# Attention's long steps in another order, and the scaling by the row sums split between ScalarE and GpSimd

## The chip, the cores and the metric

The kernel is one launch on one core of a Trainium2 chip. The metric is the device time of that launch in microseconds (us); the median of three runs of the kernel before is 765.63 us (763.31 to 770.97).

Engine names in the rows: PE is TensorE (PEld its weight loads), DVE is VectorE, ACT is ScalarE, POOL is GpSimd, SP is the engine that issues most of the DMAs (SPq its queue).

## What is computed

The reference is one attention over 16 heads (2 batches of 8, 768 positions, head size 64) whose mask comes from hashing, and behind it two feed-forward layers:

```
q_bits = (q @ proj) > 0                  # 6 bits for each row; k_bits alike
mask   = bucket(q_bits) == bucket(k_bits)
scores = where(mask, scale * q @ k.T, -1e9)
attn   = exp(scores - max(scores)) / (sum + 1e-9)
x      = attn @ v                        # 1536 rows of 512
x      = relu(x @ w_in)**2 @ w_out       # 512 -> 2048 -> 512
out    = silu(x @ w2_in) @ w2_out
```

The change lies in the attention alone: in the order of the steps that make the hash bits, and in the division of `attn @ v` by the row sums.

## The kernel before, in words

The heads are taken in 8 pairs. A pair gives 4 units (a head and one half of its 768 query rows), a unit gives 3 score tiles of 128 query rows by 768 keys. One loop, `for d in range(-5, 99)`, runs over the 96 score tiles, one for each step d, and everything is issued in the order in which it is written there: each engine works through its own list in that order and waits where an operand or a buffer is not ready. A tile that is scored in step d is reduced and put through the exponential in step d+1, transposed some steps later and multiplied with V four transposed tiles behind that. A step of the usual kind is, in order:

- VectorE: `row_max` of the last score tile (L639), `t_lo` of the last transposed tile of the step before (L678), two small operations `row_live` (L643, L644), and in some steps a piece of the preparation of four weight blocks (`w_exp`, `w_sign`, `w_low`: L597, L601, L605);
- TensorE: 6 transposes of probability blocks (`transp`, L667); ScalarE copies them out of PSUM as rounded values (`t_hi`, L672), VectorE writes the remainders (`t_lo`);
- TensorE: two times `av`, each a product of V with a rounded tile and with its remainder (L691, L692); every sixth `av` is followed by a ScalarE copy (L697) and two DMAs;
- ScalarE: the exponential of the last score tile (`score_exp`, L652);
- TensorE: the next score tile (`score_mm`, L634): four products of 384 columns, two of 128 rows and two of 76 rows. The latter hold the hash bits among their rows.

One step in twelve is a **long step** (d = 5, 17, 29, 41, 53, 65, 77). It also holds `bits_mm` of the next pair, 12 products of 384 columns (L522), and `bits_cmp` on VectorE (L527), whose result SP copies by two small DMAs into the operands of the score tiles (L558). The first score tile that needs these bits is the one that is scored two steps on. From d = 17 a long step also holds `rb_mm` (L714): 6 transposes that spread the reciprocals of the row sums of an earlier pair over 128 partitions, and `x_norm` (L723), a VectorE product of them with the pair's result. Step 92 holds `rb_mm` and `x_norm` alone. A score tile, the bits and the spread sums each take one of two PSUM buffers in turn.

At the end of a long step up to 65, ScalarE scales the queries of the pair after next (`scale_q`, L487), and GpSimd issues two DMAs of that pair (`load_hi`, L481, L482). GpSimd's list goes on with `x_put` of the normalised pair (L731 to L741), the remainders of V and of the next operands (L571, L572, L507), blocks of the weights (L614 to L623), the spreading of the next sums (L706), the sum of two halves of the result (`x_sum`, L719) and, two steps ahead of steps 5, 29, 53 and 77, the limiting of a weight block (`w_limit`, L593), which VectorE's `w_exp` in that long step reads. The feed-forward layers follow, ordered by a planner (`Plan`) that the change does not touch.

The calls in a long step:

```
extra[d0 + 5].append((bits_mm, bits_cmp, p))          # d0 = 12 * (p - 1)
extra[k].append((rb_mm, x_norm, p))                   # k = 12 * (p + 1) + 5
held = [(dve, pe(p), p) for pe, dve, p in more]       # both on TensorE at once
```

## Time and profile before

| | us |
|---|---|
| median of 3 runs (lowest, highest) | 765.63 (763.31, 770.97) |
| the profiled execution | 766.11 |
| its span, first to last instruction | 764.3 |
| TensorE busy in it | 743.0 (97%) |
| VectorE busy | 594.6 (78%) |
| ScalarE busy | 452.9 (59%) |
| GpSimd busy | 399.2 (52%) |

Attention takes about the first 255 us of the span, the feed-forward layers the rest. A busy TensorE is not one that is never held up: its products overlap, each is listed longer than the distance to the next, and short waits hide between them. The waits that matter here are read instruction by instruction in the timeline, where a bracket behind a row names the idle time ahead of it and what ended it.

### The profile page before, as it was taken

To read this page: it belongs to the slowest core of one execution; us is meant where nothing else is said; L and a number is where in the kernel's file an instruction comes from. 1 tells how busy PE (TensorE), PEld (TensorE's weight loads), DVE (VectorE), ACT (ScalarE), POOL (GpSimd) and SP (SyncE) were. 2 spreads that over 40 slices of the span, in tenths; PEclk is the share of its full clock that TensorE was granted. 3 is DMA by queue.
4 is the path that set the end of the run, shared out by engine and by line. 5 is a ranking of instruction groups with operands and counts; after the bars stand their busy time and mean duration, and the time that the engine had idled before them with its cause. 6 is when DMAs were issued, how large, how long until landed. Compare 5 with 4: busy or idle time off the path is not lost.

```text
span 764.3 us, 10886 instructions
## 1 busy us (share of the span) xinstructions
PE 743.0 (97%) x3746; PEld 630.2 (82%) x3747; DVE 594.6 (78%) x1054; ACT 452.9 (59%) x850; POOL 399.2 (52%) x290
## 2 busy tenths in 40 slices
PE   7899999999999989999999999999999999999998
PEld 3688988989988868888888888888788888888887
DVE  4789999999999799758747967899974875585542
ACT  1788888888879667367267339546634625623520
POOL 0544554864654574763564662867567255455200
PEclk8999999999999999999999999999999999999999
DMA  7787886886851402221221211202222031121012
GB/s 180 210 186 180 218 185 163 215 199 157 204 131 37 164 28 83 83 82 53 87 68 70 68 72 40 72 27 70 98 83 83 21 117 32 53 96 42 1 69 97
DMA packets 30054, 78.79 MB, mean 103 GB/s; under 512 B 4552, under 2 KB 9032, under 8 KB 30000
## 3 DMA queue, kind: packets, MB, share of 16 engines
q1 hardware_dynamic: 25808, 66.69, 30.2%
q0 software_dynamic: 4032, 11.01, 6.1%
q8 instruction: 30, 0.49, 0.3%
q10 hardware_dynamic: 160, 0.39, 0.3%
q14 instruction: 24, 0.20, 0.1%
HBM read 51.42 MB, written 3.15 MB: 71 GB/s over the span
## 4 chain that ended last, share of the span: by engine, by line
PE 76%; DVE 16%; DMA 3%; ACT 2%; issue 1%; POOL 0%; SPq 0%; ACTq 0%; DVEq 0%
PE bank L336 32%; PE bank L255 16%; PE bank L226 9%; PE s L634 6%; PE t L667 5%; DVE mt L639 3%; DVE tl L678 3%; PE o L691 3%; PE o L692 3%; PE bs L522 2%; DVE ys L149 2%; DVE xb L155 1%; ACT P L652 1%; DVE wt L173 1%; DVE wt L172 1%
## 5 line engine op out<-in xcount | busy, mean ns | idle before, releaser
L170 POOL TENSOR_SCALAR wt<-wt 128x512 f32<-128x512 f32 x56 | 116.9, 2097 | 45.3 <-ACT wt L168 45.3
L155 POOL TENSOR_TENSOR wp<-wt,wp 128x512 fp32r<-128x512 f32 x56 | 76.5, 1376 | 96.2 <-ACT wp L153 96.2
L255 PE MATMUL bank<-xb,wp 128*128 128x512 f32 x480 | 111.3, 390 | 3.8 <-DVE xb L155 2.2
L652 ACT ACTIVATE P<-s,mt 128x768 f32<-128x768 f32 x96 | 95.7, 997 | 28.3 <-DVE mt L644 25.8
L255 PEld LDWEIGHTS bank<-xb,wp 128*128 128x128 f32 x480 | 89.7, 188 | 24.0 <-DVE xb L155 2.6
L678 DVE TENSOR_TENSOR tl<-t,th 128x384 fp32r<-128x384 f32 x192 | 104.9, 548 | 3.0 <-ACT th L672 2.7
L639 DVE TENSOR_REDUCE mt<-s 128x1 f32<-128x768 f32 x96 | 91.3, 951 | 13.4 <-PE s L634 13.0
L153 ACT CAST wp<-wt 128x512 fp32r<-128x512 f32 x56 | 34.6, 620 | 105.6 <-DVE wt L173 64.4
L672 ACT CAST th<-t 128x384 fp32r<-128x384 f32 x192 | 82.2, 483 | 20.7 <-PE t L667 20.6
L634 PE MATMUL s<-kk,qq 76*128 76x384 f32 (+1 forms) x384 | 86.6, 345 | 7.4 <-DMA kk<-lp 2.9
L667 PE MATMUL t<-ident,P 128*128 128x128 f32 x576 | 81.5, 274 | 2.2 <-DVE tl L678 2.2
L260 DVE TENSOR_TENSOR ts<-bank,ts 128x512 f32<-128x512 f32 x80 | 54.7, 690 | 37.0 <-PE bank L255 34.4
L226 PE MATMUL bank<-x0h,wp 128*128 128x512 f32 x256 | 80.2, 390 | 0.0
L634 PEld LDWEIGHTS s<-kk,qq 76*128 76x128 f32 (+1 forms) x384 | 68.4, 191 | 12.0 <-issue 7.6
L667 PEld LDWEIGHTS t<-ident,P 128*128 128x128 f32 x576 | 67.7, 140 | 9.7 <-DVE tl L678 4.6
L691 PE MATMUL o<-th,vv 128*128 128x384 f32 x192 | 72.6, 378 | 0.0
L692 PE MATMUL o<-tl,vv 128*128 128x384 f32 x192 | 64.5, 336 | 0.0
L240 ACT ACTIVATE ts<-bank 128x512 f32<-128x512 f32 x48 | 28.5, 593 | 52.2 <-PE bank L226 26.7
L226 PEld LDWEIGHTS bank<-x0h,wp 128*128 128x128 f32 x256 | 48.1, 188 | 9.9
L155 DVE TENSOR_TENSOR gql<-ts,gqh 128x512 fp32r<-128x512 f32 x64 | 46.2, 733 | 12.3 <-ACT gqh L153 12.1
L172 DVE SCALAR_TENSOR_TENSOR wt<-raw,wt 128x512 uint32<-128x512 uint32 x58 | 51.5, 890 | 0.6
L168 ACT ACTIVATE wt<-raw 128x512 f32<-128x512 f32 x58 | 38.7, 670 | 20.5 <-POOL wp L155 11.0
(144 smaller groups left out, 1694.6 us busy)
## 6 DMA issues: line engine op xcount, KB each, us to landing
raw<-in_dram SPq DMA_DIRECT2D x64, 512.0 KB
qq<-hq SPq DMA_DIRECT2D x32, 192.0 KB
kk<-in_dram POOLq DMA_DIRECT2D x14, 384.0 KB, 4.8
rq<-in_dram SPq DMA_DIRECT2D x8, 384.0 KB
rk<-in_dram SPq DMA_DIRECT2D x8, 384.0 KB
qq<-lp SPq DMA_DIRECT2D x16, 192.0 KB
kk<-lp SPq DMA_DIRECT2D x16, 192.0 KB
vr<-in_dram SPq DMA_DIRECT2D x8, 384.0 KB
```

What stands on the lines that cost most here:

```text
L155: add(("DVE", "POOL")[pool], l, lambda: eng.tensor_tensor(out=lo(), in0=src(), in1=hi().bitcast(F32), op=ALU.subtract), (*rk, *hk), lk)
L170: add("DVE" if fast else "POOL", 0.5 if fast else 2.4, lambda: eng.tensor_scalar(out=wtt, in0=wtt, scalar1=W_LO, scalar2=W_HI, op0=ALU.max ...
L226: mm(bank[b], w[:, x, op, sl], t["x0"][y][:, kt], start=kt == 0 and j == 0, stop=kt == 3 and j == 2)
L255: mm(bank[b], w[:, p, op, k * 128 : k * 128 + 128], x[:, q, xop, k], start=first and k == 0 and j == 0, stop=k == 1 and j == 2, skip_group ...
L336: mm(bank[b][:, 0:wd], x, y, start=i == 0 and n == 0, stop=i == FB - 1 and n == 2)
L634: mm(s[:, n, 0:QW], t["qq"][h][0:kk, ab, c0 : c0 + 128], t["kk"][h][0:kk, ab, n * QW : (n + 1) * QW], start=ab == 0, stop=ab == 1)
L639: nc.vector.tensor_reduce(out=m[:, 0:1], in_=s[:, :, 0:QW], op=ALU.max, axis=AX.XY, negate=True)
L652: nc.scalar.activation(out=e.rearrange("p (a b) -> p a b", a=2), in_=s[:, :, 0:QW], func=AF.Exp, scale=m[:, 1:2], bias=m[:, 2:3], accum_ou ...
L667: nc.tensor.transpose(t[:, j * 128 : (j + 1) * 128], P[u, j][:, kt * 128 : (kt + 1) * 128], ident)
L678: nc.vector.tensor_tensor(out=tl, in0=t[:, 0:QW], in1=th.bitcast(F32), op=ALU.subtract)
L691: mm(o[:, 0:QW], vv, th, start=kt == 0, stop=False)
L692: mm(o[:, 0:QW], vv, tl, start=False, stop=kt == KT - 1)
```

## The change

The two PSUM buffers become two fixed tiles, and a variable says which one comes next. In a long step TensorE now takes the first `av` ahead of the bits, the next score tile straight behind the bits, then the second `av`, and `rb_mm` last, in the buffer that the bits had. Score tile and bits have the same buffers as before the change relative to one another: the score tile goes into the buffer whose exponential is done in this step. `x_norm` is no longer a VectorE product that reads PSUM; ScalarE copies the spread sums from PSUM to SBUF (into the tile `rw` from which they came), and GpSimd multiplies.

```diff
-    ps_s = att.enter_context(tc.tile_pool(name="ps_s", bufs=2, space=PSUM))
+    ps_s = att.enter_context(tc.tile_pool(name="ps_s", bufs=1, space=PSUM))
+    ss = [ps_s.tile([128, 2, 512], F32, tag=f"s{i}", name=f"s{i}") for i in range(2)]
+    parity = [0]
...
     def score_mm(u, j):
-        s = ps_s.tile([128, 2, 512], F32, tag="s", name=f"s{u}_{j}")
+        s = ss[parity[0]]
+        parity[0] ^= 1
...
     def x_norm(s, p):
-        ta = xs[p][0].rearrange("p (a b) -> p a b", a=2)
-        nc.vector.tensor_tensor(out=ta if p < 4 else x_rows(p).rearrange("p (a b) -> p a b", a=2), in0=s[:, :, 0:QW], in1=ta, op=ALU.mult)
+        rb = rows[p].rearrange("p c h d -> p (c h d)")
+        nc.scalar.copy(out=rb.rearrange("p (a b) -> p a b", a=2), in_=s[:, :, 0:QW])
+        ta = xs[p][0]
+        nc.gpsimd.tensor_tensor(out=ta if p < 4 else x_rows(p), in0=rb, in1=ta, op=ALU.mult)
...
-            held = [(dve, pe(p), p) for pe, dve, p in more]
-            for dve, t, p in held[:1]:
-                dve(t, p)
-            for n in (g - V_LAG, g + 1 - V_LAG):
-                if 0 <= n < G:
-                    av(n)
-            for dve, t, p in held[1:]:
-                dve(t, p)
+            old = [n for n in (g - V_LAG, g + 1 - V_LAG) if 0 <= n < G]
+            for n in old[0 : 1 if more else 2]:
+                av(n)
+            for pe, dve, p in more[:1]:
+                dve(pe(p), p)
             if ready and not more:
                 score_exp(*ready, m)
+            if more:
+                parity[0] ^= 1
             u, j = divmod(d + 5, 3)
             if u < NU:
                 new = u, j, score_mm(u, j)
+            if more:
+                for n in old[1:]:
+                    av(n)
+            for pe, dve, p in more[1:]:
+                dve(pe(p), p)
```

TensorE in step 41, before, from the last of the 12 products of the bits (`bs4`) to the first transpose of step 42; `rb2` are the spread sums, `o13` the two `av`, `s15_1` the next score tile:

```order
L522 MATMUL bs4_1791<-lp4_1492,pjh_92 48x384
L714 MATMUL rb2_1804<-ident_89,rw2_1700 128x128 x6
L691 MATMUL o13_1813<-th78_1711,vv3_1375 128x384
L692 MATMUL o13_1813<-tl78_1713,vv3_1375 128x384
L691 MATMUL o13_1813<-th79_1719,vv3_1375 128x384
L692 MATMUL o13_1813<-tl79_1734,vv3_1375 128x384
L634 MATMUL s15_1_1819<-kk3_1_1452,qq3_1_1451 128x384 x4
L667 MATMUL t84_1839<-ident_89,P14_0_1688 128x128
```

The same engine and step in the changed kernel, where `s0` holds first the bits and then the spread sums, and `s1` the score tile; the first two rows stand ahead of the bits:

```order
L695 MATMUL o13_1741<-th78_1663,vv3_1336 128x384
L696 MATMUL o13_1741<-tl78_1665,vv3_1336 128x384
...
L525 MATMUL s0_89<-lp4_1450,pjh_94 48x384
L638 MATMUL s1_90<-kk3_1_1411,qq3_1_1410 128x384 x4
L695 MATMUL o13_1741<-th79_1671,vv3_1336 128x384
L696 MATMUL o13_1741<-tl79_1685,vv3_1336 128x384
L718 MATMUL s0_89<-ident_91,rw2_1652 128x128 x6
L671 MATMUL t84_1787<-ident_91,P14_0_1641 128x128
```

One `av` has moved ahead of the bits, the score tile ahead of the other, and the spread sums to the end of the step.

ScalarE in the changed kernel, from the exponential of step 41 to that of step 42; before, the same list had no COPY of `rw2`:

```order
L656 ACTIVATE P15_0_1739,sums3_1439<-s1_90,mt_96 128x768
L727 COPY rw2_1652<-s0_89 128x768
L490 ACTIVATE rq5_1547<-rq5_1547 128x768
L676 CAST th84_1791<-t84_1787 128x384
L676 CAST th85_1799<-t85_1795 128x384
L656 ACTIVATE P15_1_1805,sums3_1439<-s1_90,mt_96 128x768
```

The copy of the spread sums stands ahead of `scale_q` (`rq5`), and both stand ahead of the two casts `t_hi` of step 42.

GpSimd in the changed kernel, from `x_sum` of step 39 to `x_put` of step 42; before, the same list had no product of `rw2` and `ta2`:

```order
L723 TENSOR_TENSOR ta2_1268<-ta2_1268,tb2_1269 128x768
L729 TENSOR_TENSOR ta2_1268<-rw2_1652,ta2_1268 128x768
L484 DMA hq5_1778<-rq5_1547 128x768
L485 DMA hk5_1779<-in_1_dram 128x768
L737 CAST x0h_61<-ta2_1268 128x512
```

The product stands ahead of the two DMAs of `load_hi` and of all that GpSimd does up to the next long step.

## Rows read from the trace of the kernel before

**Rows 1.** The chain that ended last, the page's shares by engine.

```profile
PE 76%; DVE 16%; DMA 3%; ACT 2%; issue 1%; POOL 0%; SPq 0%; ACTq 0%; DVEq 0%
```

**Rows 2.** Timeline of PE, score tiles of two usual steps: start, length, engine, line, operands, count.

```profile
140.01 0.86 PE L634 MATMUL s<-kk,qq 128*128 128x384 f32 x4
142.07 0.86 PE L634 MATMUL s<-kk,qq 128*128 128x384 f32 x4
```

**Rows 3.** Timeline of PE in steps 41 to 43.

```profile
124.36 0.82 PE L667 MATMUL t<-ident,P 128*128 128x128 f32 x6
125.37 0.37 PE L522 MATMUL bs<-hq,pjh 128*48 128x384 f32 x1 [0.19 <-ACT P L652]
...
127.49 0.81 PE L714 MATMUL rb<-ident,rw 128*128 128x128 f32 x6
...
128.85 0.94 PE L634 MATMUL s<-kk,qq 128*128 128x384 f32 x4
129.63 0.82 PE L667 MATMUL t<-ident,P 128*128 128x128 f32 x6
...
134.11 0.59 PE L634 MATMUL s<-kk,qq 76*128 76x384 f32 x2 [0.55 <-issue]
```

**Rows 4.** Timeline of DVE in steps 41 and 42.

```profile
127.69 1.07 DVE L527 TENSOR_SCALAR bt<-bs,pcr 48x768 fp32r<-48x768 f32 x1 [0.46 <-PE bs L522]
128.69 0.94 DVE L723 TENSOR_TENSOR ta<-rb,ta 128x768 f32<-128x768 f32 x1
...
131.35 0.55 DVE L678 TENSOR_TENSOR tl<-t,th 128x384 fp32r<-128x384 f32 x1
```

**Rows 5.** Timeline of ACT in steps 41 and 42.

```profile
127.19 0.83 ACT L487 ACTIVATE rq<-rq 128x768 f32<-128x768 f32 x1
130.21 0.86 ACT L672 CAST th<-t 128x384 fp32r<-128x384 f32 x2 [2.19 <-PE t L667]
131.47 0.99 ACT L652 ACTIVATE P<-s,mt 128x768 f32<-128x768 f32 x1 [0.39 <-DVE mt L644]
```

**Rows 6.** Timeline of PE, steps 19, 31, 55, 67: second half of the score tile.

```profile
75.97 0.59 PE L634 MATMUL s<-kk,qq 76*128 76x384 f32 x2 [0.60 <-DMA qq<-bt]
...
105.20 0.58 PE L634 MATMUL s<-kk,qq 76*128 76x384 f32 x2 [0.33 <-issue]
...
163.21 0.59 PE L634 MATMUL s<-kk,qq 76*128 76x384 f32 x2 [0.23 <-issue]
...
192.27 0.59 PE L634 MATMUL s<-kk,qq 76*128 76x384 f32 x2 [0.69 <-issue]
```

**Rows 7.** Timeline of SP in step 41, and one stretch of step 17 (DMA share, GB/s last).

```profile
129.62 0.77 SPq L558 DMA_DIRECT2D kk<-bt  x1
...
72.00:73.00 1.00, 1.00 (x9) 1.00 (x8) 1.00 (x3) 0.86 (x2) 0.92 (x2) 1.00 0.99 203
```

**Rows 8.** Timeline of POOL, steps 41 and 50 to 52.

```profile
128.43 0.59 POOL L481 DMA_DIRECT2D hq<-rq  x1 [4.74 <-PE rb L714]
...
130.38 1.29 POOL L732 TENSOR_TENSOR x0l<-ta,x0h 128x512 fp32r<-128x512 f32 x1
...
149.57 0.82 POOL L706 COPY rw<-ri 128x768 f32<-128x768 f32 x1 [1.18 <-DVE ri L704]
150.36 1.82 POOL L719 TENSOR_TENSOR ta<-ta,tb 128x768 f32<-128x768 f32 x1
152.72 1.92 POOL L593 TENSOR_SCALAR wi<-wi 128x512 f32<-128x512 f32 x1 [0.54 <-ACT wi L589]
```

**Rows 9.** Timeline of DVE in step 53.

```profile
155.01 0.42 DVE L597 TENSOR_SCALAR wi<-wi 128x512 uint32<-128x512 uint32 x1
...
157.12 1.07 DVE L527 TENSOR_SCALAR bt<-bs,pcr 48x768 fp32r<-48x768 f32 x1 [0.50 <-PE bs L522]
```

**Rows 10.** Timeline of POOL and of DVE in the feed-forward part.

```profile
276.40 2.84 POOL L155 TENSOR_TENSOR xb<-ys,xb 128x1024 fp32r<-128x1024 f32 x1
...
277.02 2.77 DVE L173 SCALAR_TENSOR_TENSOR wt<-raw,wt 128x512 uint32<-128x512 uint32 x1
```

More of the change, by code (lines that the diff above doesn't have):

```diff
@@ L516, in bits_mm @@
         t = pair[p]
-        s = ps_s.tile([128, 2, 512], F32, tag="s", name=f"bs{p}")
+        s = ss[parity[0]]
         hp, lp = t["hp"], t["lp"]
@@ L537, in bits_first @@
         t = pair[0]
-        s = ps_s.tile([128, 2, 512], F32, tag="s", name=f"bf{i}")
+        s = ss[i]
         c0 = 72 * i
@@ L629, in score_mm @@
         t = pair[p]
-        s = ps_s.tile([128, 2, 512], F32, tag="s", name=f"s{u}_{j}")
+        s = ss[parity[0]]
+        parity[0] ^= 1
         c0 = z * QW + j * 128
@@ L710, in rb_mm @@
     def rb_mm(p):
-        s = ps_s.tile([128, 2, 512], F32, tag="s", name=f"rb{p}")
+        s = ss[parity[0]]
         for c in range(6):
```

## The prediction

> **What bounds the kernel now.** I read the chain of waits first: TensorE carries 76% of it and VectorE 16% [rows 1]. Then the timeline of one usual attention step: score tiles start 2.06 us apart on TensorE [rows 2], and TensorE has nothing to wait for between them. Eight products of 384 columns and six transposes make up such a step. The twelve products of the bits start at 125.37 and the next instruction at 127.49 [rows 3], so a product takes 0.177; eight take 1.42 and six transposes the other 0.64.
>
> Then a long step, d = 41 [rows 3 to 5]. The reader should see four things. The bits wait for the exponential that frees their buffer (bracket 0.19), so the transposes end 0.37 ahead of them (124.36 + 0.64 = 125.00, bits at 125.37). The next score tile waits for `bits_cmp`: 127.69 + 1.07 = 128.76 on VectorE, and the tile, listed as 0.94 instead of 0.86, is held 0.08, to 128.93. ScalarE has 2.19 idle behind `scale_q`. And two steps on, the second half of the score tile, the half that needs the bits, waits again: bracket 0.55, with "issue" as its releaser. In step 19 the same place names the DMA `qq<-bt` [rows 6]; I take it as that DMA in all five. A listed product overlaps the next by some 0.16 (0.33 against 0.177), so the real wait is the bracket plus 0.16: 0.76 behind step 17, 0.49 behind 29, 0.71 behind 41, 0.39 behind 53, 0.85 behind 65 [rows 3, 6]. Behind step 77 no such wait stands in the timeline.
>
> So a long step is closed by a chain that TensorE's order does not set: bits, compare, small DMA, score tile. Work that is saved inside it only lengthens the wait at its end, unless the DMA comes earlier too.
>
> **The order on TensorE.** One `av` (0.35) moves into the gap ahead of the bits: 125.00 + 0.35 = 125.35, and the bits still start at 125.37. They end at 127.49; the score tile takes 4 x 0.177 to 128.20, since its buffer's exponential is over; the second `av` ends at 128.55. The spread sums wait for the compare, to 128.93, and end at 129.57. The transposes of step 42 start there instead of at 129.63 [rows 3]: 0.06 gained. The bubble has only moved from in front of the bits to in front of the spread sums.
>
> **VectorE** loses seven products of 0.94 [rows 4], 6.6 us in all. None of it is on the path by itself: in step 41 the product ran while TensorE worked on the score tile that VectorE needed next.
>
> **ScalarE** gains seven copies of 128x768 out of PSUM. No row shows one. Two casts of 384 columns out of PSUM take 0.86 together, `scale_q` over 768 columns takes 0.83, the exponential 0.99 [rows 5]. I take 0.83, the like operation without a table of exponents, and keep 0.70 and 0.99 as ends. An instruction starts some 0.07 before the listed end of the one ahead of it (128.76 and 128.69 in [rows 4]; I use the same on ScalarE). The copy starts 0.20 behind the transposes (as `bits_cmp` behind the bits), at 129.77; `scale_q`, now behind it, at 130.53; the casts of step 42 at 131.29. They were at 130.21, so they come **1.08 later**. Who waits for them: VectorE's remainder, from about 131.76 to 132.33 (0.55 long, [rows 4]), and by it the PSUM buffer that the second three transposes of step 43 take. TensorE gets there at 129.57 + 2.06 + 0.32 = 131.95 and is held until 132.35: **0.40 lost**. From there 0.32 of transposes, 0.71 of `av` and 0.35 of score tile put the half that needs the bits at 133.73. Without its wait it stood at 134.11 - 0.71 = 133.40. So what is taken from its wait is 0.71 - 0.33 = 0.38, if the DMA has landed by then.
>
> **The DMA.** In step 41 GpSimd issues the two big copies of `load_hi` from 128.43 on [rows 8], and SP issues the second small copy of bits at 129.62 [rows 7]: the small ones queue among the big ones, and in step 17 the DMA engines are 99% busy at that time [rows 7]. In the changed kernel `load_hi` stands behind the product on GpSimd. The copy ends at 130.60; the product, priced by `x_sum` of the same shape, takes 1.82 [rows 8]; so `load_hi` starts at about 132.5, **4.07 later**. The small DMAs then run almost alone, and I take it that they land by 133.7. Gains by the same sum: 0.43 behind step 17, 0.16 behind 29, 0.38 behind 41, 0.52 behind 65. Step 77 has no `scale_q` and keeps the 0.06.
>
> **GpSimd's backlog.** All that GpSimd does up to the next long step comes 4.07 later. In five periods it has several us idle before its next `rw`, and this is hidden. Between 41 and 53, where the sums of the weight blocks are made, its idle time is 1.18 ahead of `rw` and 0.54 ahead of `w_limit` [rows 8], 1.72 in all. `w_limit` is then 2.35 late: it starts at 155.07 and ends at 156.99. VectorE's `w_exp` stood at 155.01 [rows 9] and would come at some 157.07, 2.06 later; behind it on VectorE stand the remainder and `bits_cmp`, which had 0.50 to spare. `bits_cmp` is 1.56 late, and the spread sums, the bits' DMA and the score tile with it. The half in step 55 comes at 163.21 - 0.39 + 0.33 + 1.56 = 164.71: 1.50 lost, and the 0.38 of step 41 is spent waiting.
>
> **The sum**: -0.43 - 0.16 + 1.50 - 0.52 - 0.06 = +0.33. Step 5 has no `x_norm`; in step 92 the spread sums move by one `av` and the copy fits between casts: below 0.1 either way. The profiled execution took 766.11, so 766.4; the median of the runs shown lies 0.5 lower, so **766.0**.
>
> **Rivals.**
> *GpSimd is not late in step 53* (its idle time is rough, and 1.7 of 4.07 is known to be there): the 1.50 falls away and 0.44 comes in: -1.6, median scale 764.0. For it: VectorE needs `w_limit` in four long steps only, and three have idle time enough. Against: the list up to step 53 shows no other gap.
> *The bits' DMA lands no earlier*: no gain behind 17, 29, 41 and 65, and 1.56 more in step 53: +1.5, 767.1. For it: the row names "issue", not the DMA, in four of five places. Against: step 77, the one with no `load_hi`, has no wait.
> *GpSimd's product holds VectorE (slower).* One row shows such a thing: a product on words took 2.77 on VectorE while GpSimd ran one from 276.40 to 279.24, and it ended just behind it [rows 10]. If the remainder of step 42 were held like this until the product ends, at 132.5, the second transposes would slip by 0.74 in each of seven long steps: +5.2, 771.2 with the rest. It decides if the remainder cannot start beside the product. Against: the remainder at 131.35 took its usual 0.55 [rows 4] while GpSimd ran a product from 130.38 to 131.67 [rows 8].
> The Trainium skill (SBUF — State Buffer, the notes under its diagram of ports) has a rule against more work on GpSimd: it shares a pair of ports with VectorE under an exclusive lock, and a VectorE operation with two SBUF inputs waits for a whole GpSimd instruction that reads SBUF. By that rule the row at 277.02 is held and the remainder, with one input in PSUM, is not; the trace agrees with both.
>
> **Chances.** The forecast 0.52, GpSimd in time 0.20, the DMA no earlier 0.20, VectorE held 0.05, something not seen 0.03. The copy's ends move the 0.40 by -0.13 to +0.16 in five steps, -0.6 to +0.8. The runs before lay between 763.31 and 770.97, so a median of a few can be off by 1 to 2. From 764.0 less 1.4 to 767.1 plus 1.9: 762.6 to 769.0. A change of under 1% (7.7 us) can't be told from none; all waits that the change could take away make 3.2 us, so faster by that 0.02; slower only if VectorE is held for more than I priced, 0.04; within 1% 0.94.
>
> **What would show it.** `w_limit` ending behind 156 us and `w_exp` of step 53 behind it; the casts behind a long step a good 1 us later against the transposes; no wait in the second half of the score tiles of steps 19, 31, 43 and 67; `load_hi` some 4 us later. I am wrong if the remainders beside the product are longer than 0.55, if those waits stay, or if VectorE, relieved of 6.6 us, shortens the usual steps below 2.06.

## The result, and the profile after

The changed kernel took **772.71 us** (median of 12 runs, 768.9 to 777.26) beside 766.14 for the kernel before (12 runs, 763.31 to 771.22): ratio **1.0081, 95% interval 1.0062 to 1.0100**, 6.2 us slower. The forecast was 766.0 with a range of 762.6 to 769.0. A change of under 1% either way was what I held likeliest (0.94), and that came true; but the time is outside the range.

In the kernel after, `score_mm` is L638, `row_max` L643, `t_hi` L676, `t_lo` L682, `av` L695 and L696, `rb_mm` L718, `x_sum` L723, the copy on ScalarE L727, the product on GpSimd L729, V's split L574 and L575, `w_limit` L596, `w_exp` L600. Its profiled execution took 770.77, span 769.0. Of its page, the busy times and the chain by engine:

```profile
PE 745.4 (97%) x3747; PEld 630.8 (82%) x3747; DVE 591.4 (77%) x1047; ACT 457.0 (59%) x857; POOL 411.5 (54%) x297
...
PE 75%; DVE 11%; DMA 4%; POOL 3%; ACT 2%; SPq 2%; issue 2%; ACTq 0%; DVEq 0%; POOLq 0%
```

VectorE lost 5 points of the chain [rows 1], and GpSimd, which had none, has 3. That is the result in one line: work was taken from an engine with little slack and given to one that has idle time, but whose list now makes TensorE wait.

The timeline of PE in steps 41 to 43, which answers to [rows 3]:

```profile
124.51 0.82 PE L671 MATMUL t<-ident,P 128*128 128x128 f32 x6
...
125.53 0.37 PE L525 MATMUL s<-hq,pjh 128*48 128x384 f32 x1
...
127.65 0.86 PE L638 MATMUL s<-kk,qq 128*128 128x384 f32 x4
...
129.07 0.84 PE L718 MATMUL s<-ident,rw 128*128 128x128 f32 x6 [0.20 <-DVE bt L530]
129.75 0.82 PE L671 MATMUL t<-ident,P 128*128 128x128 f32 x6
...
131.80 0.49 PE L671 MATMUL t<-ident,P 128*128 128x128 f32 x3
132.55 0.55 PE L671 MATMUL t<-ident,P 128*128 128x128 f32 x3 [0.26 <-DVE tl L682]
...
133.65 0.86 PE L638 MATMUL s<-kk,qq 128*128 128x384 f32 x4
```

This stretch went as forecast. The bracket ahead of the bits is gone and stands ahead of the spread sums; the second three transposes are held (they start 0.75 behind the first three instead of 0.33, so 0.42 is lost); and the score tile of step 43 is one unbroken row of four products: the wait of 0.55 for the bits is gone, as are those of steps 19, 31, 55 and 67 [rows 6].

What went wrong is on GpSimd. ScalarE, and then GpSimd's list from step 41 on, which answers to [rows 5] and [rows 8]:

```profile
130.00 0.80 ACT L727 COPY rw<-s 128x768 f32<-128x768 f32 x1 [2.57 <-PE s L718]
130.69 0.85 ACT L490 ACTIVATE rq<-rq 128x768 f32<-128x768 f32 x1
131.44 0.85 ACT L676 CAST th<-t 128x384 fp32r<-128x384 f32 x2
```

```profile
130.94 1.84 POOL L729 TENSOR_TENSOR ta<-rw,ta 128x768 f32<-128x768 f32 x1 [7.51 <-ACT rw L727]
132.72 0.61 POOL L484 DMA_DIRECT2D hq<-rq  x1
...
147.49 0.83 POOL L574 CAST vv<-vr 128x768 fp32r<-128x768 f32 x1
148.39 1.80 POOL L575 TENSOR_TENSOR vv<-vr,vv 128x768 fp32r<-128x768 f32 x1
150.16 1.84 POOL L510 TENSOR_TENSOR lp<-rk,hk 128x768 fp32r<-128x768 f32 x1
...
152.57 0.84 POOL L710 COPY rw<-ri 128x768 f32<-128x768 f32 x1
153.36 1.85 POOL L723 TENSOR_TENSOR ta<-ta,tb 128x768 f32<-128x768 f32 x1
155.34 1.92 POOL L596 TENSOR_SCALAR wi<-wi 128x512 f32<-128x512 f32 x1
```

From 130.94 to 157.26 GpSimd does not pause. `w_limit` ends at 157.26 (forecast 156.99). But V's split, in the middle of this list, ends at 150.19, and TensorE wants V first. In the kernel before, the same split ended at 146.01:

```profile
144.18 1.83 POOL L572 TENSOR_TENSOR vv<-vr,vv 128x768 fp32r<-128x768 f32 x1
```

TensorE in steps 50 and 29, and in step 29 what it waited for on VectorE and GpSimd:

```profile
150.25 0.45 PE L695 MATMUL o<-th,vv 128*128 128x384 f32 x1 [2.73 <-POOL vv L575]
...
99.79 0.84 PE L718 MATMUL s<-ident,rw 128*128 128x128 f32 x6 [1.72 <-DVE bt L530]
```

```profile
97.04 0.43 DVE L600 TENSOR_SCALAR wi<-wi 128x512 uint32<-128x512 uint32 x1 [2.02 <-POOL wi L596]
```

```profile
93.29 1.82 POOL L723 TENSOR_TENSOR ta<-ta,tb 128x768 f32<-128x768 f32 x1 [2.97 <-DMA tb<-ob]
95.09 1.92 POOL L596 TENSOR_SCALAR wi<-wi 128x512 f32<-128x512 f32 x1
```

In step 29 the idle time that I had counted as slack was a wait for a DMA: `x_sum` stands ahead of `w_limit` and waits for `tb`. SP issued that DMA at 87.20, and it took 6.1 us to be used instead of 3.5 in the kernel before:

```profile
89.27 0.60 SPq L699 DMA_DIRECT2D tb<-ob  x1
...
92.78 1.84 POOL L719 TENSOR_TENSOR ta<-ta,tb 128x768 f32<-128x768 f32 x1 [0.53 <-issue]
```

The DMA engines are fuller at this time. DMA share and GB/s (the last two columns) of the kernel after, six us on either side of the issue, and of the kernel before, five us at the same place:

```profile
81.00:87.00 6.00, 6.00 (x42) 5.70 (x40) 5.89 (x15) 5.66 (x14) 4.65 (x4) 1.00 1.19 255
87.00:93.00 6.00, 6.00 (x41) 5.72 (x40) 5.84 (x17) 5.32 (x13) 0.82 (x1) 1.00 1.17 228
```

```profile
83.00:88.00 5.00, 5.00 (x36) 4.91 (x35) 5.00 (x12) 4.65 (x12) 0.64 (x1) 1.00 0.75 233
88.00:93.00 5.00, 5.00 (x36) 4.88 (x35) 4.96 (x16) 4.46 (x11) 1.04 (x2) 1.00 0.86 194
```

I put this down to `load_hi`, which comes late and so runs together with what is behind it. The traces show each copy landing in 16 parts. By 4.17 us behind the issue half of the parts of this `tb` had landed, instead of by 2.60 in the kernel before. In the ten traces with `load_hi` at its old place this took 2.5 to 3.4; in the ten where it came late, 3.6 to 4.7 (3.57 in b_hi2, which has the old order and the old scaling), but 2.95 in e3. So a late `load_hi` does go with a later copy. The last part can also be late alone. In b_w16 (below), with `load_hi` at its old place, 15 parts landed by 3.01 and the sixteenth at 4.26, and `x_sum` waited for it:

```profile
92.28 0.60 SPq L699 DMA_DIRECT2D tb<-ob  x1
...
97.17 1.84 POOL L719 TENSOR_TENSOR ta<-ta,tb 128x768 f32<-128x768 f32 x1 [1.91 <-DMA tb<-ob]
```

The section on the tail has what stood in front of it.

**A ledger.** The start of the same weighted sum (`av`) on TensorE, counted from the bits of step 5 and compared with the kernel before, in us (plus is later); e1 is the order alone, e2 the split alone, e8 the changed kernel with two edits (all below):

| weighted sum of step | 9 | 21 | 30 | 39 | 51 | 63 | 75 | 81 | 96 |
|---|---|---|---|---|---|---|---|---|---|
| the change | -0.12 | -0.53 | +1.07 | +1.69 | +4.34 | +4.42 | +3.94 | +4.09 | +4.61 |
| e1 | +0.17 | +0.74 | +0.69 | +0.95 | +1.13 | +1.46 | +1.42 | +2.25 | +2.32 |
| e2 | -0.32 | -1.18 | -1.09 | -0.62 | +0.64 | +1.13 | +0.18 | +0.83 | +1.06 |
| e8 | -0.11 | -0.53 | +0.74 | +1.29 | +0.95 | +2.58 | +2.07 | +2.77 | +3.29 |

The last weighted sum is 4.6 us later, and the part behind it is longer by 1.58 (511.14 instead of 509.56 to the end): 6.2 together, the 0.81% of the runs. The stretch ahead of step 5 is left out: ScalarE waits there for a weight block's DMA, and TensorE behind it, by anything from nothing to 5 us in the profiles of this study. b_w16 had it longest:

```profile
37.79 0.66 ACT L589 ACTIVATE wi<-raw 128x512 f32<-128x512 f32 x1 [5.02 <-DMA raw<-in_dram]
```

So single profiles of two kernels are compared from step 5 on. Even then a row is good to some us only: e14 (below) differs from e8 by three warm-up products ahead of step 5, and its last entry is +6.72 where e8's is +3.29.

### The profile page after: what moved, and what is told of

Read it like the earlier page. It is cut to its first block, busy times and chain, and to the rows that moved or that the text cites. A ratio compares the mean times of both kernels' runs of the same rounds, so it can differ in the third digit from the quotient of the medians.

```text
span 769.0 us, 10902 instructions
## 1 busy us (share of the span) xinstructions
PE 745.4 (97%) x3747; PEld 630.8 (82%) x3747; DVE 591.4 (77%) x1047; ACT 457.0 (59%) x857; POOL 411.5 (54%) x297
## 4 chain that ended last, share of the span: by engine, by line
PE 75%; DVE 11%; DMA 4%; POOL 3%; ACT 2%; SPq 2%; issue 2%; ACTq 0%; DVEq 0%; POOLq 0%
PE bank L336 32%; PE bank L255 17%; PE bank L226 8%; PE t L671 5%; PE s L638 5%; PE o L695 2%; PE o L696 2%; DVE ys L149 2%; PE s L525 2%; DVE tl L682 2%; DVE mt L643 1%; DMA kk<-lp 1%; DVE xb L155 1%; DVE bt L530 1%; DMA raw<-in_dram 1%
## 5 line engine op out<-in xcount | busy, mean ns | idle before, releaser
L682 DVE TENSOR_TENSOR tl<-t,th 128x384 fp32r<-128x384 f32 x192 | 104.6, 547 | 10.7 <-ACT th L676 10.4
L643 DVE TENSOR_REDUCE mt<-s 128x1 f32<-128x768 f32 x96 | 91.2, 950 | 11.9 <-PE s L638 10.9
L638 PE MATMUL s<-kk,qq 76*128 76x384 f32 (+1 forms) x384 | 85.3, 343 | 5.6 <-DMA kk<-lp 3.4
L676 ACT CAST th<-t 128x384 fp32r<-128x384 f32 x192 | 82.7, 488 | 6.7 <-PE t L671 6.7
L638 PEld LDWEIGHTS s<-kk,qq 76*128 76x128 f32 (+1 forms) x384 | 68.7, 191 | 9.4 <-issue 5.4
L695 PE MATMUL o<-th,vv 128*128 128x384 f32 x192 | 72.8, 379 | 2.7 <-POOL vv L575 2.7
L696 PE MATMUL o<-tl,vv 128*128 128x384 f32 x192 | 64.5, 336 | 0.0
```

The lines of the kernel that those rows point to most:

```text
L638: mm(s[:, n, 0:QW], t["qq"][h][0:kk, ab, c0 : c0 + 128], t["kk"][h][0:kk, ab, n * QW : (n + 1) * QW], start=ab == 0, stop=ab == 1)
L643: nc.vector.tensor_reduce(out=m[:, 0:1], in_=s[:, :, 0:QW], op=ALU.max, axis=AX.XY, negate=True)
L676: nc.scalar.copy(out=th, in_=PT[g][0][:, 0:QW])
L682: nc.vector.tensor_tensor(out=tl, in0=t[:, 0:QW], in1=th.bitcast(F32), op=ALU.subtract)
L695: mm(o[:, 0:QW], vv, th, start=kt == 0, stop=False)
```

## The experiments

Three theories: **1**, GpSimd's late and longer list; **2**, the order on TensorE; **3**, ScalarE's copy in front of the casts.

### The two halves

e1, the order alone (against the changed kernel), and e2, the split alone (the kernel before with the new `x_norm`):

```diff
 # e1, in x_norm
-        nc.scalar.copy(out=rb..., in_=s[:, :, 0:QW])
-        nc.gpsimd.tensor_tensor(out=..., in0=rb, in1=ta, op=ALU.mult)
+        nc.vector.tensor_tensor(out=..., in0=s[:, :, 0:QW], in1=ta, op=ALU.mult)
```

> The new order of the long step alone: the scaling by the sums is VectorE's product out of PSUM again, as before. Theory 1 (the loss is GpSimd's: its list starts late behind ScalarE's copy and is longer by the product): within 1 us of the kernel before, 765.3 to 767, no wait for V in step 50 and no wait for w_limit in step 29. Theory 2 (the order on TensorE costs it, rb's transposes being last in the step): 770 to 773, near the changed kernel. Theory 3 (ScalarE's copy and what stands behind it on ScalarE): 765 to 767 as well.

> The copy on ScalarE and the product on GpSimd alone, in the order of the long step before. Theory 1: slower by 3 to 7 us (769 to 773), with GpSimd's list late in the same steps, the wait for V in step 50 between 1 and 3 us and waits for w_limit in steps 29, 53 or 77. Theory 2: as before, 765 to 767. Theory 3: 768 to 772, but with the time in waits for the casts on ScalarE, and none for GpSimd.

Measured: e1 768.77 (ratio 1.0044, 1.0023 to 1.0064), e2 769.03 (1.0039, 1.0016 to 1.0063). Neither half is free. e2 came as theory 1 expects, at the low end, with a wait of 1.42 for V, and VectorE waiting 0.61 and 1.12 for `w_limit` in steps 29 and 77; no wait for ScalarE's casts is in it that the kernel before did not have, which is against theory 3. e1 lies above what theory 1 gave it and below theory 2, so neither theory alone is the whole. In e1 no wait for V or `w_limit` is left, as expected, but TensorE is held behind every long step. DVE and PE of e1 in step 42:

```profile
130.24 0.96 DVE L727 TENSOR_TENSOR ta<-s,ta 128x768 f32<-128x768 f32 x1 [1.08 <-PE s L718]
```

```profile
132.67 1.10 PE L671 MATMUL t<-ident,P 128*128 128x128 f32 x6 [0.46 <-DVE tl L682]
```

The spread sums are last in the step, so VectorE stands idle for 1.08 until they are there, and the maximum and the remainder queue behind the product. Before, the product followed `bits_cmp` at once [rows 4]. There are six such holds, with brackets of 0.40 to 0.46. A bracket leaves out the overlap of two listed products; by the starts, a hold is 0.76 to 0.82 (0.20 of it ahead of the second three transposes), 4.7 in all. In return the waits for the bits two steps on, 3.2 before, are down to 0.5, because TensorE gets there later. The difference, 2.0, is most of the 2.32 of the ledger's row, and 0.83 of it comes behind step 77, where the kernel before had no such wait to lose.

That the two halves add up to the change's 1.0081 does not mean that each keeps its price in it: in the change the same hold is 0.42, since ScalarE and not VectorE takes the spread sums.

### Where GpSimd's list starts

e3 puts the product on VectorE behind ScalarE's copy; e4 issues `scale_q` and `load_hi` ahead of copy and product; e15 leaves GpSimd's product out for the first four pairs.

```diff
 # e3
-        nc.gpsimd.tensor_tensor(out=..., in0=rb, in1=ta, op=ALU.mult)
+        nc.vector.tensor_tensor(out=..., in0=rb, in1=ta, op=ALU.mult)
 # e4, ahead of the loop over more[1:]
+            if more:
+                for fn, a in [x for x in todo[d] if x[0] in (scale_q, load_hi)]:
+                    fn(*a)
+                todo[d] = [x for x in todo[d] if x[0] not in (scale_q, load_hi)]
 # e15
+        if p >= 4:
             nc.gpsimd.tensor_tensor(out=x_rows(p), in0=rb, in1=ta, op=ALU.mult)
```

> The changed kernel with its product on VectorE, out of SBUF after ScalarE's copy; GpSimd has no product. This parts the two halves of theory 1. If it is the product's own 1.84 us on GpSimd and its wait for the copy: the wait of 2.73 us for V in step 50 falls under 1 us, w_limit is no longer waited for, and the time is 766 to 769. If GpSimd's list is late because of the load of hi, which waits for the scaling of q that stands behind the copy on ScalarE: the V wait stays at 1.5 to 2.7 us and the time at 769 to 772. Theories 2 and 3: 770 to 773, since the order and ScalarE's copy are as in the changed kernel.

> The changed kernel with the scaling of q and the load of hi put ahead of the copy and the product in the long step. Theory 1 with the product as the cause: V is still about 2.7 us late in step 50 since the product still stands ahead of it; the holds for the landing of tb in steps 29 and 77 go, if the later load of hi is what crowds the DMA engines there, and the waits in the second halves of steps 19, 31 and 67 come back (0.3 to 0.7 us each): 768.5 to 771. Theory 3: the casts are waited for less by 0.4 us in each of six steps, 768 to 770, with the V wait unchanged.

> The changed kernel without GpSimd's product for the first four pairs (their rows go on unscaled; the copy on ScalarE and all else stays). GpSimd's list then starts with the load of hi, which still waits for the scaling of q behind the copy: at 131.5 instead of 132.7 in step 41's period. If the list's start and length make V's wait: 2.73 falls by about 1.2 to 1.5 us, and the time to 770 to 771.5. If V's wait is made by something else, it stays at 2.7 and the time at 772.7.

Measured: e3 776.32 (1.0142, 1.0120 to 1.0164), e4 768.35 (1.0035, 1.0015 to 1.0055), e15 771.70 (1.0075, 1.0046 to 1.0103). For V the profiles give a clean series, counted from the start of the bits of step 41:

| | `load_hi` issued | V ready | TensorE waits for V |
|---|---|---|---|
| before | 3.05 | 20.64 | none |
| e1, order alone | 3.05 | 21.89 | none |
| e2, split alone | 5.76 | 23.29 | 1.42 |
| e4 | 3.05 | 23.66 | 1.32 |
| e15, no product | 6.41 | 23.93 | 1.99 |
| the change | 7.19 | 24.67 | 2.73 |

Ready less wait, V is wanted at 21.9 where it is waited for (22.3 in e4): the kernel before had 1.3 us of slack there, and 4 us were taken. The order alone takes 1.25 of them: in e1 GpSimd's `x_put` waits 1.28 for the product that now comes last in the step. So e1 has no wait, e2 has 1.42, and the two together have 2.73. Without the product (e15) the list starts 0.78 earlier and V comes 0.74 earlier. I had expected 1.2 to 1.5; the load started 0.40 behind the end of the scaling, with a cast as its releaser. With `load_hi` at its old place and the product kept (e4), V comes 1.01 earlier. So either one alone keeps V 3.0 to 3.3 later than before, since both wait for ScalarE's copy of the spread sums; they overlap and do not add up. The time of e15 cannot be told from the change's.

Of the kernels that keep the split and the new order, e4 alone is clearly faster than the change. It is just below what theory 1 gave it and inside what theory 3 did. V's wait is half of the 2.7 that I had expected, TensorE's wait for `w_limit` is gone, and so are the five holds for the remainders (0.42 each by the starts), since the casts now stand behind the copy alone. That is what theory 3 said of the casts. Against it, the waits for the bits came back (1.55 in step 19, 0.65 in 43, 0.63 in 67). e4 together with an earlier V was not run. e3 missed: GpSimd is relieved, but TensorE waits 1.30 to 1.36 behind each long step:

```profile
137.10 1.10 PE L671 MATMUL t<-ident,P 128*128 128x128 f32 x6 [1.36 <-DVE tl L682]
```

Copy and product one behind the other on the engines that split the tiles are the dearest form of the scaling; by the ratios, the place on GpSimd saves 0.6% against it.

### V and the sum of x earlier or later on GpSimd

e5 moves V's split to d0+7, ahead of the second load of kk; e6 also `w_abs` and `w_limit` a step earlier; e7 puts V's split behind that load; e8 is e7 with `x_sum` a step later.

```diff
 # e5; in e7 and e8 the line stands below at(d0 + 7, load_head, p, 1)
-        at(d0 + 10, split_v, p)
+        at(d0 + 7, split_v, p)
 # e6 also
-        at(d0 - 2, w_abs, key)
-        at(d0 - 2, w_limit, key)
+        at(d0 - 3, w_abs, key)
+        at(d0 - 3, w_limit, key)
 # e8 also
-        at(d0 + (3 if p < NPAIR - 1 else 2), x_sum, p)
+        at(d0 + (4 if p < NPAIR - 1 else 2), x_sum, p)
```

> The changed kernel with one part of GpSimd's list moved: the split of V three steps earlier (the end of step d0+7 in place of d0+10), ahead of the sums and puts of the weights. If the wait for V in step 50 is the largest part of the loss (2.73 us in the profile of the changed kernel), it goes, and the time is 769 to 770.5. If other waits take its place (the weights' own work that now stands behind V), 771 to 773. If the loss is the order on TensorE alone, no change from the changed kernel's 772.7 beyond 1 us.

> As the run before, and GpSimd's limit of the weights and ScalarE's absolute values one step earlier, so that they stand ahead of the sum of x, which waits for the landing of tb. GpSimd's lateness as the cause: the wait of 1.72 us of rb in step 29 goes too, and the waits for w_limit in steps 53 and 77; 767.5 to 769.5, level with the order alone (768.8), since nothing of GpSimd is left on TensorE's path. If the sum of x is as late for the puts of x as w_limit was for VectorE, 769 to 771.

> The changed kernel with the split of V three steps earlier again, but this time behind the second load of kk in GpSimd's list, not ahead of it: in the run where it stood ahead, TensorE waited for kk for 1.99 us in step 26 and 3.35 us in step 74. If GpSimd's lateness is the cause and V its largest part, the wait of 2.73 us in step 50 goes without one in its place: 769 to 771. If GpSimd's list is so full that any place costs as much, 772 to 775.

> As the run before, and the sum of x one step later (d0+4), so that the limit of the weights no longer stands behind its wait for tb's landing; the load of the weights and ScalarE's part stay where they were, which cost 1.5 and 2.4 us when they were moved. Theory 1: the waits for w_limit in steps 29 and 77 (2.02 and 0.66 us) go as well, 767.5 to 769.5. If tb, which has one buffer, is then late for the next copy out, 771 or more.

Measured: e5 775.66 (1.0109, 1.0071 to 1.0147), e6 777.23 (1.0136, 1.0097 to 1.0175), e7 771.11 (1.0067, 1.0047 to 1.0087), e8 770.08 (1.0061, 1.0043 to 1.0078). In all four the wait for V in step 50 is gone. e5 and e6 missed: they are above everything that I gave them. In both my own edit pushed the load of kk back by 2.7 us, and TensorE waited for it (1.99 in step 25 and 3.35 in step 73 of e5, one step earlier than the expectation of e7 has them); in e6 the weights' own DMA was not there a step earlier, and the casts queued behind ScalarE's wait for it. e7 came 0.1 us above what theory 1 gave it, and e8 0.6 above. They lie below the change by 0.14 and 0.20%, which is less than the intervals can tell: that V's wait was worth its 2.7 us is read from the traces, and the runs do not show it by itself. e8 shows what is left. `w_limit` is in time; `x_sum` is now the one that runs while VectorE does `w_exp`. POOL and DVE in step 53:

```profile
152.33 1.94 POOL L596 TENSOR_SCALAR wi<-wi 128x512 f32<-128x512 f32 x1
154.23 1.85 POOL L723 TENSOR_TENSOR ta<-ta,tb 128x768 f32<-128x768 f32 x1
```

```profile
154.30 2.08 DVE L600 TENSOR_SCALAR wi<-wi 128x512 uint32<-128x512 uint32 x1 [0.29 <-POOL wi L596]
```

0.42 long in [rows 9], 2.08 here, and it ends at 156.38, just behind GpSimd's 156.08. The same holds in steps 29 and 77 (1.73 each), and in e10 and e14 (1.72 to 1.75). TensorE's spread sums wait 0.93, 1.67 and 0.93 for it.

### load_hi late by itself

Two edits of the kernel before: b_hi1 a step later, b_hi2 two steps, with the first `split_pair` at d0-3.

```diff
-            at(d0 - 7, load_hi, p)
+            at(d0 - 6, load_hi, p)     # b_hi2: d0 - 5
```

> The kernel before with one edit: the load of hi one step later (d0-6 in place of d0-7). The prediction held that the waits of 0.23 to 0.98 us ahead of the second half of a score tile come of the bits' small DMAs landing behind the load of hi and of kk. If so, with that load some 2.3 us later they land first, the waits in steps 19, 31, 43, 55 and 67 (0.98, 0.60, 0.33, 0.55, 0.69 in the profile of before) go, and the time is 763 to 764.5. If the later load crowds what comes behind it (tb, lp, kk<-lp), 766 to 768.

> The kernel before with the load of hi two steps later (d0-5), and the first split of the pair one step later (d0-3) so that GpSimd doesn't wait for the load. As the run before: 763 to 764.5 if only the bits' DMAs count. This is as late as in the changed kernel (some 4 us), so if that lateness by itself makes tb or lp late there, the time is 766.5 to 769 and the profile shows waits for x_sum's tb or for kk<-lp.

Measured: b_hi1 765.43 (1.0001, 0.9977 to 1.0025), b_hi2 769.87 (1.0049, 1.0021 to 1.0077). b_hi1 tells nothing: GpSimd has nothing between the two places, and `load_hi` still came 3.05 behind the bits. In b_hi2 it came at 9.15 and the waits for the bits in steps 19, 31, 43, 55 and 67 are gone: that half of the prediction holds. But the lateness has a price of its own: `kk<-lp` is late in steps 13, 37 and 61 (1.71, 0.38 and 1.75), and 1.12 is lost in step 73. The edit also moves the first `split_pair` by a step, and the two are not parted; the time is just above what I gave.

### The tail

In every kernel with the new order and 13 warm-up products the part behind attention is 1.1 to 2.6 us longer. The last `x_sum` waits there for `tb`. One packet of 16,384 bytes of the queue that the page calls "q8 instruction", an instruction load, starts 1.7 to 2.3 us behind the last weighted sum in these (2.73 in e11 alone) and 2.9 to 3.2 us behind it with the old order. The last `tb` packets end at 2.95 before and at 3.93 in e1. TensorE's list is five to seven instructions longer with the new order (7,675 to 7,677 in the traces instead of 7,670). e12 is e1 with a list that is six shorter, b_w16 the kernel before with one that is six longer:

```diff
-        warm_up(13)
+        warm_up(10)      # b_w16: 16
```

> The new order alone with three warm-up products fewer at the start (10 in place of 13), which makes TensorE's list six instructions shorter; nothing else. If the place of the instruction load in the tail is set by the length of TensorE's list: the load comes some 2.9 us after the last weighted sum instead of 1.74, behind the packets of tb; the last sum of x starts 3.3 to 3.5 us after it instead of 4.44, the stretch behind attention is 509.6 instead of 510.7, and the time 767.5 to 768. If the tail is late for another reason, the sum of x stays at 4.4 to 5.1 us and the time at 768.8.

> The kernel before with three warm-up products more at the start (16 in place of 13), so that TensorE's list is as long as with the new order. If the instruction load is the cause of the late tail, the load moves in front of tb's last packets, the last sum of x starts 4.4 to 5 us after the last weighted sum instead of 3.30, the stretch behind attention takes 510.6 to 511.1 instead of 509.56, and the time is 767 to 767.5. If not, 765.5 to 766.5 with the tail as it was; three more warm-up products themselves are some 0.6 us of TensorE's idle start.

Measured: e12 767.75 (1.0023, 1.0005 to 1.0040), b_w16 767.22 (1.0000, 0.9977 to 1.0023). SP and POOL in the tail, of e1, of e12 and of b_w16:

```profile
257.58 0.59 SPq L703 DMA_DIRECT2D tb<-ob  x1
...
260.96 1.84 POOL L723 TENSOR_TENSOR ta<-ta,tb 128x768 f32<-128x768 f32 x1 [5.42 <-DMA tb<-ob]
```

```profile
256.35 0.59 SPq L703 DMA_DIRECT2D tb<-ob  x1
...
258.63 1.91 POOL L723 TENSOR_TENSOR ta<-ta,tb 128x768 f32<-128x768 f32 x1 [4.32 <-DMA tb<-ob]
```

```profile
259.62 0.59 SPq L699 DMA_DIRECT2D tb<-ob  x1
...
263.62 1.83 POOL L719 TENSOR_TENSOR ta<-ta,tb 128x768 f32<-128x768 f32 x1 [6.04 <-DMA raw<-in_dram]
```

3.38 from issue to use in e1, 2.28 in e12, 4.00 in b_w16 (2.25 before). `x_sum` does not read the `raw` that the last row names. The landing of `tb` shows what held it: in b_w16, 15 of its 16 parts landed at 2.97 to 3.24 behind the last weighted sum and the sixteenth at 4.99, just ahead of `x_sum` at 5.05; in e1 the sixteenth came at 4.37, and before all 16 came by 3.23. So one part is held, as by one packet in front of it. The load moved to 2.93 in e12 and to 2.30 in b_w16, and the part behind attention to 509.67 and 511.32. So the traces show this cause of a late `tb` in both directions. The runs do not resolve its price. e12 came as I had given it, and is 0.21% below e1, some 1.6 us, but the intervals overlap; the same edit made e13 (below) 0.05% faster than e11, and e14 was no faster than e8. In b_w16 the tail is 1.76 longer and the ratio is 1.0000, with an interval that reaches just as far (+0.23%); what three more warm-ups do at the start isn't separated. Nor is all of the tail this: in e2 the last sum starts as in the kernel before, and the part behind attention is still 0.77 longer.

### The place of the scaling

e9 puts copy and product behind the casts of the next step. e11 is e1 with VectorE's remainder ahead of the maximum in the step behind a long one; e13 is e11 with `warm_up(10)`.

```diff
 # e9, behind t_hi(g + 1) of the next step; the long step keeps (dve, pe(p), p) in late
+            while late:
+                dve, t, p = late.pop()
+                dve(t, p)
 # e11
+            if past and 0 <= g - 1 < G:
+                t_lo(g - 1)
             if ready:
                 m = row_max(*ready)
-            if 0 <= g - 1 < G:
+            if not past and 0 <= g - 1 < G:
                 t_lo(g - 1)
...
             more = extra.pop(d, [])
+            past = len(more) > 1
```

> The changed kernel with ScalarE's copy of the sums put behind the casts of the next step, and with it the product; the scaling of q and the load of hi thereby stand ahead of both. Theory on the order: what the order alone loses (0.40 to 0.46 us a period, PE waiting for the second split because the scaling operation is the last of the step and stands ahead of the next step's casts or splits) is due to where the scaling stands, so the waits of PE for tl in steps 18, 30, 42, 54, 66 (0.26 each) go: 1.3 to 2 us off. With the later product GpSimd is as late as in the changed kernel or later, so V's wait stays at 1.3 to 3.5 us: 769 to 771.5. If the copy's place does not matter, 772 to 773.

> The new order alone (product on VectorE, as in the run e1), with one edit: in the step after a long one VectorE's split of the last tile stands ahead of the row maximum instead of behind it. If the queue on VectorE behind the scaling is what the order loses in each period, TensorE's waits of 0.40 to 0.46 us for tl go, 766 to 767 (e1: 768.8). If the wait only moves, because the exponential is then 0.55 us later and the next score tile waits for its bank, 768 to 769.

> Both edits on the new order alone. If the two are its whole price: 765 to 766.5, level with the kernel before. If the order costs something else, 767.5 or more.

Measured: e9 774.57 (1.0122, 1.0097 to 1.0146), e11 770.05 (1.0045, 1.0025 to 1.0064), e13 769.14 (1.0040, 1.0015 to 1.0065). e9 and e11 missed; e13 fell where I had put it if the order costs something else. In e9 the holds for the remainder are gone, but the next score tile takes the buffer that the copy reads, and waits longer than the hold was:

```profile
132.54 0.98 PE L638 MATMUL s<-kk,qq 128*128 128x384 f32 x4 [0.68 <-ACT rw L727]
```

In e11 the hold grew to 0.76 to 0.81: the first three transposes run, and the second three wait for the other remainder, which now stands behind the maximum. So this other order among VectorE's operations does not help; VectorE is late as a whole, by the 1.08 that it waits for the spread sums, and has no slack to win it back in one step. In e13 the tail is cured (509.48), and the hold of 0.75 to 0.81 stays.

### All together

e10 is e8 with e9's edit; e14 is e8 with `warm_up(10)`.

> The three edits together: V's split behind the second kk load three steps earlier, the sum of x one step later, the copy of the sums behind the next step's casts. If GpSimd's lateness and the place of the scaling are all that the change costs, nothing of the loss is left: 764.5 to 767, level with the kernel before or a little faster. If the order has a further price, 768 to 770.

> The changed kernel with V's split three steps earlier behind the second kk load, the sum of x one step later and three warm-up products fewer. If the causes add up: the 4.9 us that V and the sum of x left (the run e8) less the 1.1 to 1.5 us of the tail, 767.5 to 769, with the sum of x 3.3 us behind the last weighted sum. If the late start of GpSimd's list still costs in the waits for w_limit in steps 29, 53 and 77 (0.9 to 1.7 us in e8), the upper end or 769.5.

Measured: e10 772.58 (1.0097, 1.0079 to 1.0115), e14 770.78 (1.0088, 1.0057 to 1.0118). Both missed, and no version beats the kernel before. In e10 the score tile's 0.68 is back in each period. In e14 the tail is cured (`x_sum` 3.49 behind the last weighted sum), V is in time, but TensorE waits 1.90 for `kk<-in_dram` in step 25, 0.73 for `kk<-lp` in 37, and 0.83 and 0.75 for remainders in steps 52 and 53. The causes do not add up by taking them away. One reason is seen in e5 and e6: in a full list, what is moved forward makes something else late. The wait of 1.90 in e14 is not of that kind: GpSimd issues this load at the same place as in e8, 12.6 behind the bits of step 17, but it took 9.9 us to land instead of 7.5. Why is open.

## Why the prediction was wrong

**The step that failed** is the backlog: "In five periods it has several us idle before its next `rw`, and this is hidden", and for the period from 41 to 53 the price of `w_limit` alone. The size and the cause of the lateness were right (`load_hi` 4.07 later forecast, 4.14 measured). The check of who waits was too short: I looked only at the end of GpSimd's list. For `w_limit` in step 53 the sum had 1.50; in its place the ledger, taken step by step, has 2.97 for V and 1.47 for `w_limit` in step 29.

- V in step 50: not in the sum. It had 1.3 us of slack, and TensorE waited 2.73 for it. This is the largest single term.
- `w_limit` in step 29: the idle time that I counted as cover was a wait for a DMA, and that DMA took 6.1 us instead of 3.5: TensorE waited 1.72. The late `load_hi` is a part of the reason; the rest is not shown.
- `w_limit` in step 53: it ends at 157.26, and `w_exp` starts behind it, as forecast. It cost nothing more, since TensorE had already been held by V.
- The order: for the change as it stands, this term was sized rightly. I had priced the hold by ScalarE's casts at 0.40, and by the starts of the transposes it is 0.42, in each of the five steps. What the working did not follow is that the spread sums come last, so that whichever engine takes them is held until then. With VectorE's product (e1) this costs 0.44% together with the tail; in the change it also makes the copy late (4.47 behind the bits in step 41, 3.03 in e2), and so the start of GpSimd's list.
- Smaller terms, also not in the sum: `kk<-lp` in step 37 (0.36 in the bracket), and 0.59 in the ledger behind step 92, where a small VectorE operation was held (below).
- The tail: put at nothing, and 1.58 longer. It was not to be read from the profile before, except that the instruction load there starts close behind the packets of `tb`. That the load is a cause of the late sum is shown in the traces; what it is worth in the runs is not.

**What was right.** The bits' DMAs land in time and five waits go: the ledger shows -0.41 between steps 9 and 21 (forecast -0.43 behind step 17) and -0.48 between 63 and 75 (forecast -0.52 behind 65). The copy took 0.80 (0.83), the casts came 1.07 later (1.08), and the bubble moved from the bits to the spread sums. None of the three signs of being wrong that I had named appeared: they did not look at V, at `tb` or at the tail.

**The rivals.** GpSimd in time, and the bits' DMA no earlier, are refuted. The third, GpSimd's product holding VectorE, came in another place. Its time, 771.2, is the nearest to the measured one, but by luck: it was priced by the remainders, and they kept their 0.55. But an operation that reads and writes SBUF alone can be held: the small addition ahead of the reciprocals (128x12), 0.16 or 0.17 long in all eight pairs before, took 1.34 beside V's split and 1.05 beside the last product, where TensorE then waited 0.39. Of the kernel before, and then of the kernel after:

```profile
149.07 0.16 DVE L703 TENSOR_SCALAR ri<-sums 128x12 f32<-128x12 f32 x1
```

```profile
148.89 1.34 DVE L707 TENSOR_SCALAR ri<-sums 128x12 f32<-128x12 f32 x1
...
252.97 1.05 DVE L707 TENSOR_SCALAR ri<-sums 128x12 f32<-128x12 f32 x1
```

The Trainium skill (SBUF — State Buffer, SBUF: two separate sides) names, beside the operation with two SBUF inputs that I quoted, a VectorE operation in a two-port mode among those that take the shared pair; the trace agrees, if these one-input operations run in such a mode, which no row shows: 0.42 became 1.73 to 2.08 for `w_exp` in e8, and each time it ended within 0.3 us of the GpSimd instruction's end.

## What to carry to other kernels

When an engine's list starts later, follow every instruction in it to its reader, with the reader's slack (here 1.3 us for V, and the order took nearly all of it before the split took the rest), up to the point where the engine has idle time that is not itself a wait for a transfer. An operation that is put last in a step holds whichever engine takes its result and all that this engine does next; price it there, not on the engine that issues it. In a list that is full, moving one thing forward is a change of its own, with its own late readers. And a wait that is seen in a trace is not yet a time: here several edits that took one away (e7, e13, e14) gave back less in the runs than the bracket had.

## What the runs showed of the hardware

- **An instruction load can stand in a transfer's way.** A packet of 16,384 bytes took 0.9 to 1.7 us; where it started ahead of the last packets of a 96 KB copy, the copy was used 3.4 to 4.1 us after its issue instead of 2.2 to 2.4, with 15 of its 16 parts on time and one late. In step 29 of e4 such a packet, 2.10 behind the issue, held nothing. A few instructions more or fewer in TensorE's list, 250 us earlier in the program, decided it in e12 and b_w16. The Trainium skill (Runtime: NRT & Kernel Launch, Terms) says that an engine's instruction memory is refilled in blocks of 16 KiB; the page of the kernel after agrees, with 30 such packets and 0.49 MB:

```profile
q8 instruction: 30, 0.49, 0.3%
```

- **A tiny VectorE operation can wait for a whole GpSimd instruction**: 0.16 became 1.05 to 1.34 for 12 columns, and 1.83 in e2, where it ran from 145.56 to 147.39 and GpSimd's instruction from 145.52 to 147.36.
